# Windowed attention beside a gated MLP on one core: the attention of a chunk done in one piece or in two halves of its tokens

## Chip, cores and metric

The kernel runs on one core of one Trainium2 chip. The metric is the time on the device in microseconds (us); of several runs the median is taken. The time before is 718.12 us, the median of three runs (717.82 to 720.67).

## The reference

The input is one sequence of 2048 tokens of width 1024. It is normalised; the normalised tokens go through an attention with 32 heads of 32, in which each token looks at itself and the seven tokens at distances 2, 4, ... 14 before it, and through a gated MLP of inner width 3584. The output is the input plus attention times silu of the MLP.

```python
qkv = (xn @ wqkv)                       # 3 x 32 heads x 32
W, dil = 8, 2
idx = pos[:, None] - off[None, :]       # off = 0, 2, ... 14
logits = jnp.einsum("bhsd,bhswd->bhsw", q, kg) * scale
logits = jnp.where(mask[None, None, :, :], logits, -1e9)
attn = _softmax(logits, axis=-1)
o = jnp.einsum("bhsw,bhswd->bhsd", attn, vg)
s = o @ wo
g = _silu((_silu(xn @ w1) * (xn @ w3)) @ w2)
return x + s * g
```

## The kernel before

The tokens are worked on in two blocks of 1024, each of two chunks of 512, so there are four chunks (0 to 3). TensorE (PE) does the projections, the MLP and the output projection. Each of these products is a two by two block product done with seven instead of eight partial products, which costs VectorE (DVE) many sums and differences of weights, of inputs and of results; the ones of the first block's MLP weights are kept in HBM (s_dram, t_dram) and loaded again for the second block.

The order of the blocks is: projections q, k, v (qkv_first, qkv_pairs), up projections in 14 steps (up_step), attention of the block's first chunk, down projection (mlp_down), output projection of that chunk (wo). The attention of the block's second chunk stands at the start of the next block, or at the end of the program, and its output projection after the next block's projections. Queries, keys or values that come before they can be used are parked in HBM (put, get).

That is the order in which the operations are written down. The order on each engine is made by a planner (class Plan, lines 43 to 247): each operation is noted with its engine, what it reads and writes, and an assumed cost; PE keeps the written order, and for the other engines `limits` works back from PE to the time by which each operation is due, and `simulate` takes on each engine, whenever it is free, the ready operation that is due first. `plan.lift` moves the due times of a group: for chunks 1 to 3 the softmax and its copies are pulled forward by 60 us (SOFT, line 699). Buffers of a pool are handed out in the written order (`place`, line 72). So a change of the attention can move DVE, ScalarE (ACT) and the DMA queues of SyncE (SP) and GpSimd (POOL), but not PE. An engine runs its list in order: an instruction that waits holds up everything behind it.

The attention of a chunk c (`attention`, line 701) does not use PE. Queries, keys and values lie with the 128 partitions as 32 heads times 4 parts of a head's width, and 8 further values (j) in the free dimension, each for 512 tokens: `qo[:, u, j, :]`, `kT`, `vT`; keys and values have the last 16 tokens of the chunk before in front (HALO, copied by `halo`, line 547).

- Scores (lines 709 to 726): for each of the 8 distances w, the product of q and the shifted k in two instructions of 2048 elements (four j each, `qk`), the sum of the two (`qa`, 2048), then sums of halves (`qb`, 1024; `qc`, 512) into a tile E that holds, for each of four quarters of the tokens, 8 distances of 128 tokens. What is left to sum is across the four partitions of a head.
- Regrouping (lines 734 to 738): four DMAs of 256 KB, two issued by POOL and two by SP, copy E into L so that a partition holds one head and one quarter of the tokens, with the four parts side by side. L takes two of the three buffers of the pool `att`.
- Softmax (lines 739 to 762): three sums of 1024 fp32 elements (`z`), a tree of three maxima (512, 256, 128; `tr`), the difference (`zd`, 1024), the exponential on ACT (line 756, 1024), a tree of three sums, a reciprocal (line 760, 128) and the product (`pb`, 1024).
- Spreading (lines 763 to 766): four DMAs of 256 KB copy the weights back into E, for each of the four partitions of a head.
- Product with v (lines 768 to 792): for each half of the j, 8 products and 7 sums of 2048 elements (`pv`, `pa`), over q in `qo`.

All `tt` operations (sums, products) are recorded at line 365, all copies on ACT at 370, silu at 373, all DMAs at 379, and the matmuls at 356 (some of the down projection at 1070). In the profile att is the pool of attention buffers, k the fp32 buffers for results of PE, mm the banks of PSUM, r the large buffers for weights.

Of the kernel before, what the change touches and what calls it, by code (L numbers as in the profile page):

```python
# [8 lines left out]
FP32 = mybir.dt.float32  # L9
BF16 = mybir.dt.bfloat16  # L10
FP16 = mybir.dt.float16
ACTF = mybir.ActivationFunctionType
ALU = mybir.AluOpType

PE, DVE, ACT, POOL, SP = range(5)
# [229 lines left out]
def kernel(  # L245
# [11 lines left out]
    nc = tc.nc  # L257
    P = 128
    S, D, F = 2048, 1024, 3584
    Dh, W, DIL = 32, 8, 2  # L260
    KT = D // P
    KH = KT // 2
    CH = 512
    BL = 1024
    NB = S // BL
    NST = CH // P
# [3 lines left out]
    HALO = 16  # L270
    NJ = 8
    NR = 4
    NQ = 7
    scale = float(Dh) ** -0.5
# [10 lines left out]
    const = ctx.enter_context(tc.tile_pool(name="const", bufs=1))  # L285
# [11 lines left out]
    maskb = const.tile([P, W, HALO], BF16, name="maskb")  # L297
    kT = const.tile([P, NJ, HALO + CH], BF16, name="kT")
    vT = const.tile([P, NJ, HALO + CH], BF16, name="vT")
    h_sb = const.tile([P, FT, BL], BF16, name="h_sb")  # L300
    h16 = h_sb[:].bitcast(FP16)
    E = const.tile([P, NST, W, P], BF16, name="E")
    qo = const.tile([P, 2, NJ, CH], BF16, name="qo")
    xT = const.tile([P, 2, KT, CH], BF16, name="xT")
    xT16 = xT[:].bitcast(FP16)
# [4 lines left out]
    plan = Plan()  # L310
# [15 lines left out]
        out=ident[:], in_=ident[:], compare_op=ALU.not_equal, fill=1.0,  # L326
# [4 lines left out]
        out=maskb[:], in_=maskb[:], compare_op=ALU.is_ge, fill=-1.0e9,  # L331
# [2 lines left out]
    nc.gpsimd.memset(kT[:, :, 0:HALO], 0.0)  # L334
    nc.gpsimd.memset(vT[:, :, 0:HALO], 0.0)
    warm = plan.pools["k2"][7][:].bitcast(BF16)
    zero = E[:, 0, 0:4, :].rearrange("p w n -> p (w n)")
    nc.vector.memset(warm[:, 0:CH], 0.0)
    nc.vector.memset(zero, 0.0)
    for i in range(12):  # L340
# [22 lines left out]
    def tt(name, fn, o, a, b, rd, wr, n, fast, late=0.0):  # L363
        occ = n / (1920.0 if fast else 960.0) + 0.068
        plan.op(DVE, name, lambda: fn(out=o(), in0=a(), in1=b()), rd, wr, occ, 0.08, late=late)  # L365

    add, sub, mul, mx = (nc.vector.tensor_add, nc.vector.tensor_sub, nc.vector.tensor_mul, nc.vector.tensor_max)
# [8 lines left out]
    def dma(eng, name, o, a, rd, wr, kb, run=1024, late=0.0):  # L376
        e = {SP: nc.sync, POOL: nc.gpsimd, ACT: nc.scalar}[eng]
        occ = {SP: 0.45, POOL: 0.58, ACT: 0.55}[eng]
        plan.op(eng, name, lambda: e.dma_start(out=o(), in_=a()), rd, wr, occ, 0.0, nbytes=kb * 1024, late=late, run=run)  # L379
# [20 lines left out]
    def qo_cells(u, js, gs=range(4)):  # L400
        return [("qo", u, j, g) for j in js for g in gs]
# [297 lines left out]
    SOFT = (0.0, -60.0, -60.0, -60.0)  # L699

    def attention(c):
        u = c % 2
        J4 = [range(0, 4), range(4, 8)]
        r4 = lambda s: s.ap().rearrange("p (j n) -> p j n", j=4)
        if ("q", c) in park:
            get(c, "q")
        if ("k", c) in park:
            halo("k")
            get(c, "k")
        for w in range(W):  # L710
            o = HALO - DIL * w
            pr = []
            for jh in range(2):
                p_t = plan.slot("att", f"p{c}_{w}_{jh}")
                tt(f"qk{c}", mul, lambda p_t=p_t: r4(p_t), lambda jh=jh: qo[:, u, jh * 4:jh * 4 + 4, :],
                   lambda jh=jh, o=o: kT[:, jh * 4:jh * 4 + 4, o:o + CH],
                   qo_cells(u, J4[jh]) + [("k", j) for j in J4[jh]] + ([("k", j, "halo") for j in J4[jh]] if w else []),
                   [p_t], 2048, True)
                pr.append(p_t)
            p0, p1 = pr  # L720
            tt(f"qa{c}", add, lambda p0=p0: r4(p0), lambda p0=p0: r4(p0), lambda p1=p1: r4(p1), [p0, p1], [p0], 2048, True)
            tt(f"qb{c}", add, lambda p0=p0: r4(p0)[:, 0:2], lambda p0=p0: r4(p0)[:, 0:2], lambda p0=p0: r4(p0)[:, 2:4],
               [p0], [p0], 1024, True)
            tt(f"qc{c}", add, lambda w=w: E[:, :, w, :], lambda p0=p0: r4(p0)[:, 0].rearrange("p (q n) -> p q n", n=P),
               lambda p0=p0: r4(p0)[:, 1].rearrange("p (q n) -> p q n", n=P),
               [p0], [("E", w, sq) for sq in range(4)], 512, True)
        if ("v", c) in park:
            halo("v")
            get(c, "v")
        if c == 0:  # L730
            tt("mask", add, lambda: E[:, 0, :, 0:HALO], lambda: E[:, 0, :, 0:HALO], lambda: maskb[:],
               [("E", w, 0) for w in range(W)], [("E", w, 0) for w in range(W)], 128, False)
        plan.lift = SOFT[c]
        L = plan.slot("att", f"L{c}", 2)
        Lv = lambda r: L.ap().rearrange("p (r w n) -> p r w n", r=NR, w=W)[:, r]
        for sq in range(4):
            dma((POOL, SP)[sq % 2], f"L{c}", lambda sq=sq: L.ap()[sq:P:4].rearrange("h (r n) -> h r n", r=NR),
                lambda sq=sq: E[:, sq].rearrange("p w n -> p (w n)"), [("E", w, sq) for w in range(W)], [(L, sq)], 330, 2048)
        zf = lambda s: s.ap().bitcast(FP32)
        z = plan.slot("att", f"z{c}")  # L740
        zv = lambda: zf(z).rearrange("p (w n) -> p w n", w=W)
        LC = [(L, sq) for sq in range(4)]
        tt(f"z{c}", add, zv, lambda: Lv(0), lambda: Lv(1), LC, [z], 1024, False)
        tt(f"z{c}", add, zv, zv, lambda: Lv(2), LC + [z], [z], 1024, False)
        tt(f"z{c}", add, zv, zv, lambda: Lv(3), LC + [z], [z], 1024, False)
        zm = plan.slot("att", f"zm{c}")
        zt = lambda s: zf(s)[:, 0:512].rearrange("p (w n) -> p w n", w=4)

        def tree(t, op):
            tt(f"tr{c}", op, lambda: zt(t), lambda: zv()[:, 0:4], lambda: zv()[:, 4:8], [z], [t], 512, False)  # L750
            tt(f"tr{c}", op, lambda: zt(t)[:, 0:2], lambda: zt(t)[:, 0:2], lambda: zt(t)[:, 2:4], [t], [t], 256, False)
            tt(f"tr{c}", op, lambda: zt(t)[:, 0:1], lambda: zt(t)[:, 0:1], lambda: zt(t)[:, 1:2], [t], [t], 128, False)

        tree(zm, mx)
        tt(f"zd{c}", sub, zv, zv, lambda: zt(zm)[:, 0:1].to_broadcast([P, W, P]), [z, zm], [z], 1024, False)
        plan.op(ACT, f"exp{c}", lambda: nc.scalar.activation(out=zf(z), in_=zf(z), func=ACTF.Exp, scale=scale),  # L756
                [z], [z], 1.07, 0.11, table="exp")
        zs = plan.slot("att", f"zs{c}")
        tree(zs, add)
        plan.op(DVE, f"rec{c}", lambda: nc.vector.reciprocal(out=zt(zs)[:, 0], in_=zt(zs)[:, 0]), [zs], [zs], 0.87)  # L760
        pb = plan.slot("att", f"pb{c}")
        pbv = lambda: pb.ap()[:, 0:1024].rearrange("p (w n) -> p w n", w=W)
        tt(f"pb{c}", mul, pbv, zv, lambda: zt(zs)[:, 0:1].to_broadcast([P, W, P]), [z, zs], [pb], 1024, False)
        for sq in range(4):
            dma((POOL, SP)[sq % 2], f"E{c}", lambda sq=sq: E[:, sq].rearrange("p w n -> p (w n)"),
                lambda sq=sq: pb.ap()[sq:P:4, 0:1024].unsqueeze(1).to_broadcast([32, NR, 1024]),
                [pb], [("E", w, sq) for w in range(W)], 330, 2048)
        plan.lift = 0.0
        for jh in range(2):
            js = slice(jh * 4, jh * 4 + 4)  # L770
            A = lambda js=js: qo[:, u, js, :]
            Ac = qo_cells(u, J4[jh])

            def pv(dst, wr, w, jh=jh, js=js):
                o = HALO - DIL * w
                q4 = lambda a: a.rearrange("p j (q n) -> p j q n", n=P)
                tt(f"pv{c}", mul, lambda: q4(dst()), lambda: E[:, :, w, :].unsqueeze(1).to_broadcast([P, 4, NST, P]),
                   lambda: q4(vT[:, js, o:o + CH]),
                   [("E", w, sq) for sq in range(4)] + [("v", j) for j in J4[jh]]
                   + ([("v", j, "halo") for j in J4[jh]] if w else []), wr, 2048, True)  # L780

            pv(A, Ac, 0)
            B = plan.slot("att", f"B{c}")
            pv(lambda B=B: r4(B), [B], 1)
            tt(f"pa{c}", add, A, A, lambda B=B: r4(B), Ac + [B], Ac, 2048, True)
            for w0 in (2, 4, 6):
                B, C = plan.slot("att", f"B{c}"), plan.slot("att", f"C{c}")
                pv(lambda B=B: r4(B), [B], w0)
                pv(lambda C=C: r4(C), [C], w0 + 1)
                tt(f"pa{c}", add, lambda B=B: r4(B), lambda B=B: r4(B), lambda C=C: r4(C), [B, C], [B], 2048, True)  # L790
                tt(f"pa{c}", add, A, A, lambda B=B: r4(B), Ac + [B], Ac, 2048, True)


    def xn_sums(hold=False):
# [515 lines left out]
    for st in range(NST):  # L1310
        x_load(0, st, x0)
    plan.op(ACT, "warm", lambda: nc.scalar.activation(out=scr[:], in_=eps_t[:], func=ACTF.Sqrt), [], [], 0.2,
            table="sqrt")
# [125 lines left out]
```

## Time and profile before

| | |
|---|---|
| median of three runs | 718.12 us (717.82 to 720.67) |
| the profiled execution | 718.92 us, span of its instructions 716.9 us |
| PE busy | 706.6 us, 3407 matmuls |
| DVE busy | 661.9 us, 901 instructions |
| ACT busy | 389.4 us, 668 instructions |
| DMA | 150.56 MB, mean 210 GB/s |
| DVE on the attention's tile att | 313.9 us |
| copies E to att, att to E | 32 of 256 KB, 2.4 to 7.3 us from issue to landing |

The span runs from the first to the last instruction; what is around it (2.0 us) is start and end of the execution. An engine's busy time counts each moment once, also where two instructions overlap. A group's line gives the number of instructions, their total, the mean of one in ns, and the idle time of the engine just before them with what ended it. A timeline's line gives start, length, engine, line, operation, tiles, shape and how many, and in brackets the idle time before.

The four chunks' attention lies so in the trace (first to last instruction on DVE): chunk 0 from 48.0 to 246.8 us, chunk 1 from 244.4 to 414.5, chunk 2 from 414.4 to 552.0, chunk 3 from 547.3 to 689.1.

### The profile page before, as it was taken

What the parts mean: (1) busy time and instruction counts of PE and PEld (TensorE: products, weight loads), DVE (VectorE), ACT (ScalarE), POOL (GpSimd) and SP (SyncE); (2) the same over time, 40 slices, a digit from 0 to 9 for tenths busy, and PEclk for the clock granted to TensorE, in tenths of its full rate; (3) what the DMA queues carried; (4) which work ended last, traced back from release to release, by engine and by line L of the source; (5) the groups of instructions that cost most, each with busy time, mean ns of one, the idle gap of its engine ahead of it and who ended that gap; (6) DMA issues with size and microseconds to landing.
All of it is one profiled execution on the core that took longest, in us unless ns stands there. A gap on an engine that the chain in (4) does not pass through costs nothing.

```text
span 716.9 us, 9340 instructions
## 1 busy us (share of the span) xinstructions
PE 706.6 (99%) x3407; PEld 352.3 (49%) x3462; DVE 661.9 (92%) x901; ACT 389.4 (54%) x668; POOL 25.4 (4%) x54
## 2 busy tenths in 40 slices
PE   8999999999999999999999999999999999999997
PEld 5655544444444444744555554444444444455443
DVE  6999999987999999979799999975999997999968
ACT  6755465567565697534535354657565654422233
POOL 0011100100000000000000000000000000000000
PEclk9999999999999999999999999999999999999999
DMA  8579985866544849695554559897537346437523
GB/s 315 214 247 388 370 295 167 283 207 215 183 169 150 305 127 241 144 299 184 192 156 157 176 183 321 267 307 225 194 109 254 113 157 213 155 128 239 177 73 103
DMA packets 127262, 150.56 MB, mean 210 GB/s; under 512 B 12400, under 2 KB 104176, under 8 KB 122864
## 3 DMA queue, kind: packets, MB, share of 16 engines
q1 hardware_dynamic: 113312, 121.58, 52.3%
q0 software_dynamic: 5312, 26.22, 9.3%
q10 hardware_dynamic: 8592, 2.16, 2.2%
q8 instruction: 27, 0.44, 0.3%
q14 instruction: 19, 0.16, 0.1%
HBM read 106.95 MB, written 32.51 MB: 195 GB/s over the span
## 4 chain that ended last, share of the span: by engine, by line
PE 97%; DVE 1%; DMA 1%; issue 1%; SPq 0%; DVEq 0%
PE mm L356 93%; PE mm L1070 3%; DVE r L365 1%; DMA r<-in_A_wqkv_dram 1%; PE mm L508 0%; SPq L379 0%; DVEq L1434 0%; DVEq L365 0%
## 5 line engine op out<-in xcount | busy, mean ns | idle before, releaser
L356 PEld LDWEIGHTS <-r 128*128 128x128 f16 (+1 forms) x2288 | 239.9, 107 | 245.8 <-DMA r<-in_A_wqkv_dram 2.3
L356 PE MATMUL mm<-xs,r 128*128 128x512 f16 x1280 | 295.2, 379 | 0.0
L356 PE MATMUL mm<-xT,r 128*128 128x512 bf16 (+1 forms) x968 | 224.4, 369 | 3.4 <-DMA r<-in_A_wqkv_dram 1.3
L370 ACT COPY k<-mm 128x512 f32<-128x512 f32 (+1 forms) x200 | 115.0, 579 | 87.0 <-PE mm L356 73.0
L356 PE MATMUL mm<-r,h_sb 128*128 128x512 bf16 (+1 forms) x694 | 153.7, 379 | 0.5
L365 DVE TENSOR_TENSOR att<-att 128x2048 bf16<-128x2048 bf16 (+4 forms) x132 | 124.0, 950 | 7.2 <-ACT att L756 5.2
L356 PEld LDWEIGHTS <-h_sb 128*128 128x128 f16 (+1 forms) x800 | 78.2, 98 | 93.2
L370 ACT COPY mm<-mm 128x512 f32<-128x512 f32 (+1 forms) x92 | 51.5, 563 | 81.7 <-PE mm L356 69.5
L365 DVE TENSOR_TENSOR att<-qo,kT 128x2048 bf16<-128x2048 bf16 x64 | 76.8, 1215 | 0.0
L365 DVE TENSOR_TENSOR att<-E,vT 128x2048 bf16<-128x2048 bf16 x56 | 66.2, 1216 | 0.0
L365 DVE TENSOR_TENSOR h_sb<-mm,k 128x512 bf16<-128x512 f32 x96 | 62.8, 680 | 0.9 <-PE mm L356 0.3
L365 DVE TENSOR_TENSOR r<-r,r 128x1024 f16<-128x1024 bf16 (+6 forms) x76 | 58.9, 784 | 1.9 <-DMA r<-in_A_wqkv_dram 1.3
L373 ACT ACTIVATE k<-k 128x512 bf16<-128x512 f32 x56 | 34.7, 630 | 45.1 <-DVE k L365 45.0
L365 DVE TENSOR_TENSOR k<-mm,k 128x512 f32<-128x512 f32 x72 | 47.8, 683 | 9.8 <-PE mm L356 9.5
L365 DVE TENSOR_TENSOR h_sb<-h_sb,k 128x1024 bf16<-128x1024 bf16 x56 | 37.0, 683 | 14.0 <-ACT k L370 14.0
L373 ACT ACTIVATE h_sb<-mm 128x512 bf16<-128x512 f32 x60 | 35.8, 598 | 18.1 <-PE mm L356 18.0
L370 ACT CAST k<-mm 128x512 bf16<-128x512 f32 x56 | 32.5, 587 | 12.4 <-PE mm L356 12.4
L365 DVE TENSOR_TENSOR qo<-qo,att 128x2048 bf16<-128x2048 bf16 x32 | 38.9, 1215 | 0.0
L365 DVE TENSOR_TENSOR h_sb<-h_sb 128x512 f16<-128x512 bf16 (+1 forms) x72 | 37.4, 561 | 1.0 <-DMA h_sb<-in_B_w_dram 0.8
L365 DVE TENSOR_TENSOR r<-r 128x1024 f16<-128x1024 bf16 (+2 forms) x36 | 27.8, 790 | 0.6 <-DMA r<-t_dram 0.6
L356 PE MATMUL mm<-h_sb 128*128 128x512 f16 x96 | 22.4, 379 | 0.1
L373 ACT ACTIVATE xs<-k 128x512 bf16<-128x512 f32 x8 | 5.0, 630 | 20.6 <-DVE k L365 20.6
(98 smaller groups left out, 378.9 us busy)
## 6 DMA issues: line engine op xcount, KB each, us to landing
r<-in_B_w_dram SPq DMA_DIRECT2D x42, 512.0 KB, 4.0
s_dram<-r POOLq DMA_DIRECT2D x14, 1024.0 KB, 5.5
r<-t_dram SPq DMA_DIRECT2D x16, 896.0 KB, 6.6
r<-s_dram SPq DMA_DIRECT2D x14, 1024.0 KB, 4.9
r<-in_A_wqkv_dram SPq DMA_DIRECT2D x11, 1024.0 KB, 6.8
r<-in_B_w_dram SPq DMA_DIRECT2D x12, 896.0 KB, 4.7
h_sb<-in_B_w_dram SPq DMA_DIRECT2D x14, 512.0 KB, 11.2
t_dram<-h_sb POOLq DMA_DIRECT2D x14, 512.0 KB, 6.9
```

Source lines behind the costliest of these rows:

```text
L356: nc.tensor.matmul(cut(ps.ap()), lhsT=lhs[k](), rhs=cut(rhs[k]()), start=(first and k == 0), stop=(last and k == n - 1), skip_group_check= ...
L365: plan.op(DVE, name, lambda: fn(out=o(), in0=a(), in1=b()), rd, wr, occ, 0.08, late=late)
L370: plan.op(ACT, name, lambda: nc.scalar.copy(out=o(), in_=a()), rd, wr, occ, 0.11)
L373: plan.op(ACT, name, lambda: nc.scalar.activation(out=o(), in_=a(), func=ACTF.Silu), rd, wr, occ, 0.11, table="silu")
L1070: nc.tensor.matmul(ps.ap()[:, col * 256:(col + 1) * 256], lhsT=lhs[k](), rhs=r()[:, k, :], start=first and k == 0, stop=False, skip_group_ ...
```

## The change

The attention of a chunk is done for the first 256 tokens and for the second 256, one behind the other in each step: scores and regrouping of half 0, scores and regrouping of half 1; softmax and spreading of half 0, then of half 1; product with v of half 0, then of half 1. E has the shape [P, 2 halves, 4 quarters of a half, W, 64]. A product of scores takes all 8 j of 256 tokens at once (2048 elements), so its sums have 1024, 512 and 256 elements. L takes one buffer for each half; the softmax of a half works on 512 columns and keeps its intermediate results in one buffer. The copies have 128 KB each, in contiguous runs of 1 KB, and there are twice as many.

```diff
-    E = const.tile([P, NST, W, P], BF16, name="E")
+    E = const.tile([P, 2, 4, W, CH // 8], BF16, name="E")
...
-        for w in range(W):
...
-                tt(f"qk{c}", mul, lambda p_t=p_t: r4(p_t), lambda jh=jh: qo[:, u, jh * 4:jh * 4 + 4, :],
...
-            tt(f"qa{c}", add, lambda p0=p0: r4(p0), lambda p0=p0: r4(p0), lambda p1=p1: r4(p1), [p0, p1], [p0], 2048, True)
...
+        tok = [slice(h * HN, (h + 1) * HN) for h in H2]
...
+        for h in H2:
+            for w in range(W):
+                p = plan.slot("att", f"p{c}_{w}_{h}")
+                kw, kc = kv("k", w, h)
+                pj = lambda a, b, p=p: (lambda: r8_(p)[:, a:b])
+                tt(f"qk{c}", mul, pj(0, 8), lambda h=h: qo[:, u, :, tok[h]], kw, qc_(h) + kc, [p], 2048, True)
+                tt(f"qa{c}", add, pj(0, 4), pj(0, 4), pj(4, 8), [p], [p], 1024, True)
+                tt(f"qb{c}", add, pj(0, 2), pj(0, 2), pj(2, 4), [p], [p], 512, True)
+                row = lambda j, p=p: (lambda: r8_(p)[:, j].rearrange("p (q n) -> p q n", q=4))
+                tt(f"qc{c}", add, lambda w=w, h=h: E[:, h, :, w, :], row(0), row(1), [p], ec(h, [w]), 256, True)
...
+            plan.lift = SOFT[c]
+            L.append(plan.slot("att", f"L{c}_{h}"))
+            for q in Q4:
+                dma((POOL, SP)[q % 2], f"L{c}",
...
+                    lambda q=q, h=h: E[:, h, q].rearrange("p w n -> p (w n)"), ec(h, q=[q]), [(L[h], q)], 165, 1024)
+            plan.lift = 0.0
...
-        L = plan.slot("att", f"L{c}", 2)
...
-        tt(f"z{c}", add, zv, lambda: Lv(0), lambda: Lv(1), LC, [z], 1024, False)
...
-        for sq in range(4):
-            dma((POOL, SP)[sq % 2], f"E{c}", lambda sq=sq: E[:, sq].rearrange("p w n -> p (w n)"),
...
+        for h in H2:
...
+            tt(f"z{c}", add, zv, Lv(0), Lv(1), LC, [zz], 512, False)
+            tt(f"z{c}", add, zv, zv, Lv(2), LC + [zz], [zz], 512, False)
+            tt(f"z{c}", add, zv, zv, Lv(3), LC + [zz], [zz], 512, False)
...
+            tree(mx)
+            tt(f"zd{c}", sub, zv, zv, wide, [zz], [zz], 512, False)
+            plan.op(ACT, f"exp{c}", lambda zf=zf: nc.scalar.activation(out=zf(0, 512), in_=zf(0, 512), func=ACTF.Exp, scale=scale),
+                    [zz], [zz], 0.6, 0.11, table="exp")
+            tree(add)
+            plan.op(DVE, f"rec{c}", lambda zf=zf: nc.vector.reciprocal(out=zf(512, 576), in_=zf(512, 576)), [zz], [zz], 0.47)
...
+            for q in Q4:
+                dma((POOL, SP)[q % 2], f"E{c}", lambda q=q, h=h: E[:, h, q].rearrange("p w n -> p (w n)"),
+                    lambda q=q, pbv=pbv: pbv()[q:P:4].unsqueeze(1).to_broadcast([32, NR, 512]),
+                    [zz], ec(h, q=[q]), 165, 1024)
         plan.lift = 0.0
-        for jh in range(2):
...
+        for h in H2:
+            A = lambda h=h: qo[:, u, :, tok[h]]
...
```

The planner makes a new order from this. On PE it is the same as before. On DVE 898 planned operations become 1042. On ACT the eight exponentials of 512 elements stand one by one between other work in chunks 0, 2 and 3, each with a load of its table before it and of silu's after it; in chunk 1 the two stand together.

## The prediction

> **What bounds it now.** I read the totals of the page first, then the chain of work that ended last, then the waits of TensorE (PE) alone, and only then VectorE (DVE), on which the whole change lies.
>
> ```profile
> PE 706.6 (99%) x3407; PEld 352.3 (49%) x3462; DVE 661.9 (92%) x901; ACT 389.4 (54%) x668; POOL 25.4 (4%) x54
> ...
> PE 97%; DVE 1%; DMA 1%; issue 1%; SPq 0%; DVEq 0%
> ```
>
> ```profile
> PE mm L356 <- DMA r<-in_A_wqkv_dram: 1.3, 2, 0.9
> PE mm L341 <- DVE k L338: 1.2, 1, 1.2
> PE mm L508 <- DVE r L443: 0.3, 1, 0.3
> ```
>
> The second fence is the complete list of what PE waits for: 2.8 us, all in the first stages. The chain names PE from 25 us to the last matmul at 712.2 us, in stretches without a hole, and the granted clock is 1.00 in every window up to 700 us. So PE sets the end, and neither attention nor anything else of DVE holds it up anywhere. A time saved on DVE has nowhere to go; a time added on DVE costs nothing as long as each result still comes before the matmul that needs it.
>
> What the change can fill is idle time of DVE. The timeline of DVE shows where it stood:
>
> ```profile
> 475.28 0.69 DVE L365 TENSOR_TENSOR h_sb<-h_sb,k 128x1024 bf16<-128x1024 bf16 x1 [4.24 <-ACT k L370]
> ...
> 488.06 1.16 DVE L365 TENSOR_TENSOR att<-att 128x512 f32<-128x512 f32 x2 [3.02 <-ACT att L756]
> ...
> 499.45 0.69 DVE L365 TENSOR_TENSOR h_sb<-h_sb,k 128x1024 bf16<-128x1024 bf16 x1 [4.19 <-ACT k L370]
> ```
>
> These three are chunk 2: attention is blocked first on the regrouping copies (issued 468.1, used 475.9), then on the exponential, then on the spreading copies (issued 492.9, used 500.9), and DVE has too little else to do. All of DVE's gaps of over 1 us between 60 us and the last attention instruction at 689.1 come to 31.7 us. PE waited in none of them.
>
> **The change, part by part.** PE's instructions and their order are the same, one by one; so are the sums, the stores and the loads of weights. What changes is on DVE, ACT and the queues of SP and POOL.
>
> *Scores.* Durations come from the groups kept apart by shape:
>
> ```profile
> L365 DVE TENSOR_TENSOR att<-qo,kT 128x2048 bf16<-128x2048 bf16 x64 | 76.8, 1215 | 0.0
> L365 DVE TENSOR_TENSOR att<-att 128x1024 bf16<-128x1024 bf16 x32 | 21.7, 681 | 0.0
> L365 DVE TENSOR_TENSOR E<-att 128x512 bf16<-128x512 bf16 x32 | 13.1, 415 | 0.0
> L365 DVE TENSOR_TENSOR r<-r,xs 128x256 bf16<-128x256 bf16 x2 | 0.5, 282 | 0.0
> L365 DVE TENSOR_TENSOR att<-att 128x1024 f32<-128x1024 f32 x12 | 14.7, 1222 | 0.3
> L365 DVE TENSOR_TENSOR att<-att 128x512 f32<-128x512 f32 x8 | 5.5, 684 | 5.2 <-ACT att L756 5.2
> ```
>
> Before, a chunk takes 16 products of 1.215 us and 8 times (1.215 + 0.681 + 0.415): 37.9 us. After, the same 16 products and 16 times (0.681 + 0.415 + 0.282): 41.5 us. Same elements, 24 instructions more. These durations overlap, though: two independent instructions of 1.215 us take 2.35 us, so each starts 80 ns before the end of the one ahead. Net +3.6 - 24 x 0.08 = **+1.6 us** per chunk. The rows hold no run of 64 elements spread over four dimensions; but weight sums that step in runs of 4 take 1.218 us for 2048 elements and the products with v in runs of 128 take 1.216, so I price the new shapes by size alone.
>
> ```profile
> 579.99 2.35 DVE L365 TENSOR_TENSOR att<-qo,kT 128x2048 bf16<-128x2048 bf16 x2
> ...
> 477.63 2.48 DVE L365 TENSOR_TENSOR att<-att 128x1024 f32<-128x1024 f32 x2
> ```
>
> *Softmax.* Before: 5 x 1.22, two trees of 0.684 + 0.420 + 0.286, a reciprocal of 0.948: 9.8 us. After: 10 x 0.684, four trees of 0.420 + 0.286 + 0.22 (the last an estimate from the 286 ns of 128 and the 420 ns of 256), two reciprocals of 0.55 (estimated from 948 ns at 128 and 154 ns at 1): 11.6 us. Less 12 overlaps of 0.08: **+0.85 us**. The second line above is a pair in which the second reads what the first wrote: 2.48 is 2 x 1.222 + 0.03, so a dependent neighbour loses 0.11 us. By the printed order attention has 20 such neighbours before and 31 after: +1.3 us in all, **+0.3** per chunk.
>
> *Product with v.* Still 30 instructions of 2048 elements a chunk: 0.
>
> Sum: 2.75 us a chunk, 11 us in all, of which DVE has 55 free. It lies beside PE's matmuls. Two dates decide whether it stays there. The second chunk's attention ends at 414.5; the first sum that needs all of it precedes its matmul (423.5) by 7.3 us, so it may end at 421.8. The fourth ends at 689.1; the next sum started at 696.6, held by matmuls of the chunk before it, with 2.0 us to spare, so it may end at 698.6. If no gap were filled at all, two chunks' extra (5.5 us) put these ends at 420.0 and 694.6: still in time. With gaps filled they come earlier than now. So **0** on the path. Without this cover the whole 11 us would show.
>
> *Exponential.* Four become eight, each with half the elements: 0.63 us by the 512-element activations beside 1.056. In the changed order chunks 0, 2 and 3 load the tables twice, chunk 1 once as now: 6 loads more.
>
> ```profile
> 485.68 1.28 ACT L756 ACT_TABLE_LOAD   x1
> 486.98 1.06 ACT L756 ACTIVATE att<-att 128x1024 f32<-128x1024 f32 x1
> ...
> 489.50 1.28 ACT L373 ACT_TABLE_LOAD   x1
> ```
>
> A detour now costs ACT 2 x 1.283 + 1.056 = 3.6 us, and the evictions behind this one still came 0.7 us before their matmul at 492.6. A new one is 3.2 us, with other work between the two: **0**, at most 3.2 + 3.2 - 3.6 - 0.7 = 2.1 us a chunk if two fall together. [...]
>
> *Copies.* L and E go in 64 DMAs of 128 KB instead of 32 of 256 KB: 16 more issues on SP (0.59 us each) and 16 more on POOL (0.56). They land 2.4 to 7.3 us after the issue now. Stores of 256 KB take 2.4 and of 128 KB 1.8, so a half could land 0.6 us sooner; behind a 512 KB weight load it lands no sooner. I take the same latency, and 0. On SP, in chunk 1, four copies of L now stand ahead of a load from t_dram that had one ahead of it and one behind; such loads land 4.7 us or more ahead of use, against three issues more (1.8 us). Elsewhere a copy waits at the head of SP until its half is done, with weight loads behind it; the tightest of these have 1.6 us. [...]
>
> *Start and tail.* DVE's order is the same up to 48 us, and the last 28 us have the same instructions. Nothing to gain there.
>
> The profiled execution took 718.92 us (span 716.9, and 2.0 around it), 0.8 over the median of the three runs, 718.12. With 0 on the path and 0.3 for margins that shrink, the median should be **718.4**.
>
> **The rivals.**
>
> *DVE comes late and PE waits (slower).* For it: windows 200:250, 350:450 and 650:675 are full; the smallest margins of DVE ahead of a matmul are 0.3 us at 301.1, 1.3 at 289.8 and 1.75 at 449.4. Against it: the priority work stands in the same places, and attention fills between. It decides when the halved instructions don't overlap. If all 36 added ones of a chunk cost 0.182 us (0.068 plus 0.114) and nothing is filled, a chunk takes 6.7 more: the ends are 427.9 and 702.5, late by 6.1 and 3.9, which gives 729. At half of that (4.7 a chunk) the ends are 423.9 and 698.5: 2.1 late, 720.5. I put it at 724.
>
> *ACT's detours fall together.* Three chunks by 2.1 us: 725. Against it: DVE work of a half lies between two exponentials.
>
> *A copy holds up weight loads on SP.* The half that is waited for is late by DVE's own delay; one such wait past the 1.6 us margin, by the 4 us a load takes to land: 718.4 + 2.4, about 721.
>
> *Faster.* The gaps are filled and the ends of attention come earlier; PE needs neither. Only a hole in PE could give time back, and after 25 us there is none: 718.0 at best. That the planner does not lay the halves behind each other (chunk 1's L copies all stand together) ends in the forecast's time too.
>
> **How the numbers follow.** A difference of 0.5% (3.6 us) is about what this measurement can tell from none. Forecast and its equal-time rivals 0.72; DVE late 0.15; ACT 0.06; SP 0.04, all three counted as slower; faster by over 0.5% 0.03. The range runs from 717.4 (0.4 under the fastest run shown, 717.8, which is about how far the two faster ones lie apart) to 724.0, the middle of the first rival.
>
> **What would show it.** Right: PE's list of waits stays under 4 us, the chain stays 97% PE, DVE's busy time is 671 to 675 us in about 1045 instructions, 7 table loads of the exponential instead of 4, the idle time of DVE around 475, 488 and 499 shrinks, and it grows before 694. Wrong: a wait of PE for DVE h_sb, k or mm at line 365, or for ACT k or mm at line 370; halved shapes over their price; copies that land after 8 us.

## The result, and the profile after

The changed kernel takes 742.64 us in the median of 4 runs (741.49 to 744.57), the kernel before 718.71 (717.82 to 720.67) beside it: a ratio of 1.034, with a 95% interval of 1.031 to 1.037. The forecast was 718.4 us with a range up to 724.0. It was wrong by 24 us, on the side to which it gave a quarter of the chance.

The totals of the page after, and its chain of the work that ended last:

```profile
PE 713.7 (96%) x3407; PEld 354.3 (48%) x3462; DVE 671.3 (90%) x1045; ACT 389.5 (52%) x678; POOL 34.2 (5%) x70
...
PE 8%; DVE 4%; issue 0%; DVEq 0%
```

DVE is busy 671.3 us in 1045 instructions, as forecast. But its share falls from 92 to 90%, since the span has grown by 25.1 us, from 716.9 to 742.0. The chain no longer runs back through PE to the start: it covers the last 12% of the span and breaks off. All of PE's waits (total us, times, longest):

```profile
PE mm L356 <- ACT k L370: 12.4, 3, 9.2
PE mm L1074 <- DVE mm L365: 4.0, 3, 2.8
PE mm L356 <- DVE h_sb L365: 1.7, 3, 0.7
PE mm L341 <- DVE k L338: 1.2, 1, 1.2
PE mm L508 <- DVE r L443: 0.7, 1, 0.7
PE mm L356 <- DMA r<-in_A_wqkv_dram: 0.6, 1, 0.6
```

They come to 20.6 us where there were 2.8. PE is also busy 7.1 us longer (706.6 to 713.7) with the same matmuls. The waits have grown by 17.8 us; 17.8 and 7.1 are 24.9 of the 25.1 us, so two questions are left: why PE waits, and why its work takes longer.

The largest wait leads to the first one's cause. These are rows of the timelines of chunk 0, engine by engine (start, length, instruction, and in brackets the idle time before and what ended it):

```profile
155.39 0.69 DVE L365 TENSOR_TENSOR att<-att 128x512 f32<-128x512 bf16 x1 [5.87 <-DMA att<-E]
158.80 3.19 DVE L365 TENSOR_TENSOR att<-att 128x512 f32<-128x512 f32 x6 [2.72 <-DMA att<-E]
...
175.93 0.29 DVE L365 TENSOR_TENSOR att<-att 128x128 f32<-128x128 f32 x1 [3.29 <-DMA E<-att]
179.00 0.22 DVE L365 TENSOR_TENSOR att<-att 128x64 f32<-128x64 f32 x1 [2.77 <-DMA E<-att]
```

```profile
149.54 7.10 SPq L379 DMA_DIRECT2D att<-E  x2
```

```profile
156.37 0.55 POOL L379 DMA_DIRECT2D att<-E  x1 [6.01 <-DVE att L365]
```

```profile
158.77 1.28 ACT L764 ACT_TABLE_LOAD   x1 [7.42 <-DMA att<-E]
```

```profile
165.09 3.55 PE L356 MATMUL mm<-xs,r 128*128 128x512 f16 x8 [9.18 <-ACT k L370]
...
181.61 3.10 PE L356 MATMUL mm<-xs,r 128*128 128x512 f16 x8 [2.62 <-ACT k L370]
```

The instruction at 155.39 is the first sum of half 0's softmax. It needs half 0's four L copies, the last of which had landed at 148.61 (landings are taken from the trace, by each copy's semaphore). It started 0.28 us after the landing of two copies of *half 1*, issued at 149.54 and 149.81 (landed 154.78 and 155.11). The other two copies of half 1 then were issued at 156.10 and 156.37, as soon as that sum had ended at 156.08: SP's two issues took 7.10 us, and POOL's row names DVE as what it waited for. The second sum, at 158.80, followed the landing of those two (158.72). So a sum of half 0 waits for copies of half 1, copies of half 1 for that sum, and the next sum for these copies. None of this is in the data. At 175.93 and 179.00 the same happens with the spreading: the tree of half 1 waits for the E copies of half 0, which only read half 0's result. In chunk 2 the three idle times that the prediction showed around 475, 488 and 499 us (4.24, 3.02 and 4.19 us, ended by ACT) have given way to three that a copy ends: 2.69 us before 488.74, 4.70 before 506.43 and 2.30 before 509.16.

What is common to all of them is the tile. L, the softmax's intermediate results and the spread source all lie in the one wide tile att, in different thirds of it, and a copy touches every fourth partition of its third (`[q:P:4]`). The planner keeps its own books by buffer and lays half 0's sums beside half 1's copies; the waits in the program follow the order in which these come out and the tile. In the kernel before, no copy of a chunk stands between two parts of the chunk's softmax, so nothing there could wait in this way.

### The profile page after: what moved, and what is told of

Its sections match the earlier page's. It is cut to its first block, busy times and chain, and to the rows that moved or that the text cites. A ratio compares the mean times of both kernels' runs of the same rounds, so it can differ in the third digit from the quotient of the medians.

```text
span 742.0 us, 9547 instructions
## 1 busy us (share of the span) xinstructions
PE 713.7 (96%) x3407; PEld 354.3 (48%) x3462; DVE 671.3 (90%) x1045; ACT 389.5 (52%) x678; POOL 34.2 (5%) x70
## 5 line engine op out<-in xcount | busy, mean ns | idle before, releaser
L356 PEld LDWEIGHTS <-r 128*128 128x128 f16 (+1 forms) x2288 | 240.7, 108 | 262.8 <-issue 20.6
L356 PE MATMUL mm<-xs,r 128*128 128x512 f16 x1280 | 298.5, 382 | 14.2 <-ACT k L370 12.4
L365 DVE TENSOR_TENSOR att<-att 128x1024 bf16<-128x1024 bf16 (+8 forms) x240 | 133.4, 589 | 33.1 <-DMA E<-att 16.7
L370 ACT COPY k<-mm 128x512 f32<-128x512 f32 (+1 forms) x200 | 113.4, 580 | 76.4 <-PE mm L356 59.6
L370 ACT CAST k<-mm 128x512 bf16<-128x512 f32 x56 | 32.3, 590 | 8.3 <-PE mm L356 8.0
L379 POOL DMA_DIRECT2D att<-E x16 | 8.8, 557 | 312.2 <-DVE E L365 306.2
```

The costliest lines, as they stand in the source:

```text
L356: nc.tensor.matmul(cut(ps.ap()), lhsT=lhs[k](), rhs=cut(rhs[k]()), start=(first and k == 0), stop=(last and k == n - 1), skip_group_check= ...
L370: plan.op(ACT, name, lambda: nc.scalar.copy(out=o(), in_=a()), rd, wr, occ, 0.11)
```

## The experiments

Each ran beside the kernel before on the same chip; the ratios are to that kernel.

| kernel | us, median | ratio, 95% interval | PE's waits, us |
|---|---|---|---|
| after | 742.64 | 1.034 (1.031 to 1.037) | 20.6 |
| e1: three tiles for att | 719.17 | 1.0019 (1.0010 to 1.0028) | 4.0 |
| e2: copies of both halves together | 719.00 | 1.0013 (1.0003 to 1.0024) | 2.6 |
| e2a: only the L copies together | 726.17 | 1.0115 (1.0101 to 1.0129) | 7.4 |
| e3: exponential off the softmax | 739.92 | 1.0304 (1.0288 to 1.0319) | 20.3 |
| e4: scores alone in halves | 719.24 | 1.0018 (1.0002 to 1.0034) | 2.0 |
| e5: wide tile, blocks of partitions | 727.30 | 1.0132 (1.0118 to 1.0146) | 9.6 |
| e6: three tiles and blocks | 726.30 | 1.0099 (1.0079 to 1.0119) | 9.8 |
| e7: before, with blocks | 722.11 | 1.0048 (1.0033 to 1.0063) | 4.5 |

**e1, three tiles.** My theory was now the false waits; the rivals were the amount of work on DVE, the table loads, and the number of copies. One line tells them apart, since it moves no instruction:

```diff
-    plan.wide = {"att": (const.tile([P, 12 * CH], BF16, name="att"), 4 * CH)}
+    plan.pools["att"] = [const.tile([P, 4 * CH], BF16, name=f"att{i}") for i in range(3)]
```

> The changed kernel with the three buffers of att as three tiles in place of one wide one; every instruction stands in the same place on every engine, and only waits differ. Theory 1 (false waits: a copy between E and one buffer of the wide tile att is taken to touch the whole tile, so that the softmax of one half waits for the other half's copies): PE's waits fall from 18 to under 4 us, PE busy from 713.7 to about 707, 718 to 721 us. Theory 2 (too much work on DVE, halved instructions and dependent neighbours) and theory 3 (table loads of the exponential between PE's evictions) change nothing here: 738 us or more. Theory 4 (twice as many copies of half the size clog the queues): also 735 or more.

Measured 719.17 us. The same first sum of half 0, on DVE's timeline of this run:

```profile
149.98 0.69 DVE L365 TENSOR_TENSOR att<-att 128x512 f32<-128x512 bf16 x1 [0.41 <-DVE E L365]
```

It starts 5.4 us earlier, 0.2 us after the landing of half 0's own last L copy (149.80); the copies of half 1, which land from 156.16 on, no longer hold it. PE's busy time is back at 706.9 us. All of the loss but 1.4 us is gone (0.0019 of 718; 0.7 to 2.0 by the interval), with every added instruction, table load and copy still there: the three rivals together explain no more than that rest. The order on DVE, ACT and POOL is the changed kernel's, instruction by instruction.

**e2, copies together.** The wide tile stays, and the order is changed instead:

```diff
-            LC = [(L[h], q) for q in Q4]
+            LC = [(L[x], q) for x in (H2 if h == 0 else (1,)) for q in Q4]
...
+            z.append(zz)
+        for h in H2:
+            pbv = lambda zz=z[h]: zz.ap()[:, 1536:2048]
             for q in Q4:
...
-                    [zz], ec(h, q=[q]), 165, 1024)
+                    z, ec(h, q=[q]), 165, 1024)
```

> The wide tile stays, but the copies of the two halves are put together: the first sum of half 0 is planned behind all L copies, and the E copies of both halves behind both halves' softmax. Shapes, instruction counts, eight exponentials, 64 copies of 128 KB as in the changed kernel. Theory 1: no copy lies between the softmax of the two halves, so nothing is left to wait for falsely: 718 to 722 us, PE's waits under 5 us. Theories 2 and 4: 735 or more. Theory 3: between, since two exponentials may share a load of their table.

Measured 719.00 us (ratio 1.0013). Here half 0's first sum waits for all eight L copies, more than in the changed kernel, and all changes together cost 0.9 us (0.2 to 1.7 by the interval). The wait itself is not what is dear: the planner now knows of it and gives DVE other work, which in chunk 0 lies between 149.9 us and that sum's start at 158.0. The loss goes here with the wide tile where it was, so the buffers' place in memory is not its cause either.

**e2a, one side only.** The first line of that diff alone.

> As the run before, but only the L copies are put together; the E copies of half 0 still start before half 1's softmax is over, so that the false waits on the spreading side stay and those on the regrouping side go. Theory 1: the stall of 9.2 us on PE near 165 us goes, stalls of up to 3 us as at 181 us may stay in each of chunks 0 to 3: 719 to 730 us. Theories 2 to 4: 735 or more.

Measured 726.17 us, and on DVE's timeline the two waits of the spreading side are still there:

```profile
177.09 0.42 DVE L365 TENSOR_TENSOR att<-att 128x256 f32<-128x256 f32 x1 [3.94 <-DMA E<-att]
180.15 0.55 DVE L365 TENSOR_TENSOR att<-att 128x128 f32<-128x128 f32 x2 [2.63 <-DMA E<-att]
```

So the regrouping side costs 742.6 - 726.2 = 16.5 us and the spreading side 726.2 - 719.0 = 7.2. The planner's order differs a little between these kernels, so this is a division of the loss, not an exact price of each wait.

**e3, exponential off the softmax.** PE waited for ACT, and ACT stood 7.42 us at the exponential's table load. I took that for the way by which DVE's delay reached PE.

```diff
-            ... nc.scalar.activation(out=zf(0, 512), in_=zf(0, 512), func=ACTF.Exp, scale=scale),
+            ... nc.scalar.activation(out=scr[:], in_=scr[:], func=ACTF.Exp, scale=scale),
```

> The changed kernel in the same order, but the exponential works on one column that nothing else uses, so the scores are not exponentiated: the eight table loads stay, and nothing on ScalarE waits for the softmax any more. DVE's false waits stay. If PE stalls because ScalarE stands in line behind the exponential with PE's evictions behind it (theory 1, by way of ScalarE): PE's wait for ACT k falls from 12.4 to under 2 us, and the time to 721 to 730 us. If the stall reaches PE by DVE's own late work: 735 or more. If the table loads themselves cost the time (theory 3): 740.

Measured 739.92 us: what I had taken for the way (721 to 730 us) was wrong. By itself this time would also fit the price of the table loads (740), but e1 keeps all of them and had ruled that out. PE's waits changed their name:

```profile
PE mm L356 <- DVE h_sb L365: 13.3, 5, 6.9
PE mm L1074 <- DVE mm L365: 3.8, 3, 2.4
```

DVE's false waits stay: it stands 5.95 us before the first sum of half 0 at 155.91 us and 3.17 before the next at 159.78. Behind these, in the order of the changed kernel and of e1, stands a sum into h_sb that starts at 167.75 us (at 158.68 in e1), and PE waits 6.94 us for DVE's h_sb, until 168.48. Freed from the one road, the delay comes by the other. The wait on ACT adds some 2 to 3 us to it at most (742.6 - 739.9; the intervals of the ratios touch).

**e4, scores alone.** The kernel before with only the scores in halves (products of 8 j by 256 tokens, the rest as it was).

```diff
+        for h in range(2):
+            for w in range(W):
+                o = HALO - DIL * w + h * 256
+                p = plan.slot("att", f"p{c}_{w}_{h}")
...
+                tt(f"qc{c}", add, lambda w=w, h=h: E[:, 2 * h:2 * h + 2, w, :], row(0), row(1), [p],
+                   [("E", w, 2 * h), ("E", w, 2 * h + 1)], 256, True)
```

> The kernel before with the scores alone in halves: products of 8 j by 256 tokens, sums of 1024, 512 and 256 elements (24 instructions more a chunk, +1.6 us a chunk on DVE); regrouping, softmax, spreading and product with v as before, 32 copies of 256 KB, no copy between two parts of a softmax. The prediction's price of this part on the path is 0: 717.5 to 720 us, DVE busy 666 to 671 us, PE's waits under 4 us. If more and smaller instructions on DVE cost by themselves: 722 or more.

Measured 719.24 us, with DVE busy for 668.2 us in place of 661.9: 6.3 us more, 1.6 a chunk. PE's waits (2.0 us) show nothing of it on the path; by the ratio it costs 1.3 us, and 2.4 at most.

**e5, blocks of partitions.** If the tile is at fault, which part of it? This kernel keeps the wide tile and the order and changes only how a copy walks over its partitions. The softmax works row by row, so it does not matter which row a head's quarter takes.

```diff
-                    lambda q=q, l=L[h]: l.ap()[q:P:4].rearrange("h (r n) -> h r n", r=NR),
+                    lambda q=q, l=L[h]: l.ap()[32 * q:32 * q + 32].rearrange("h (r n) -> h r n", r=NR),
...
-                    lambda q=q, pbv=pbv: pbv()[q:P:4].unsqueeze(1).to_broadcast([32, NR, 512]),
+                    lambda q=q, pbv=pbv: pbv()[32 * q:32 * q + 32].unsqueeze(1).to_broadcast([32, NR, 512]),
```

> The changed kernel with the one wide tile, the same order on every engine and the same copies, but a copy's 32 partitions of att are a block (32q to 32q+31) in place of every fourth (q, q+4, ...); the softmax works row by row, so the output is the same. If it is the strided walk over partitions that makes a copy seem to touch all three buffers (theory 1 in full): as with three tiles, 718 to 721 us, PE's waits under 4 us. If the wide tile alone does it, whatever the walk: 738 us or more. If the copies land later because a block of partitions moves slower than a strided set, the median from issue to landing rises above 4.5 us (E to att) or 3 us (att to E); without false waits that stays hidden.

Measured 727.30 us: between the two. The pattern of chunk 0 is gone (PE's stall there is 1.2 us in place of 9.2), so the walk matters. But I had written that slower copies would stay hidden, and they did not. The DMA lists of e1 and of e5 (KB each, median us from issue to landing), and e5's first wait of PE:

```profile
att<-E SPq DMA_DIRECT2D x16, 128.0 KB, 3.6
att<-E POOLq DMA_DIRECT2D x16, 128.0 KB, 4.5
```

```profile
att<-E SPq DMA_DIRECT2D x16, 128.0 KB, 6.9
att<-E POOLq DMA_DIRECT2D x16, 128.0 KB, 6.5
```

```profile
PE mm L356 <- DMA r<-in_A_wqkv_dram: 4.3, 2, 3.9
```

From E to att, a block of 32 partitions lands 2.0 to 3.3 us later than every fourth one. In chunk 1, SP then issued the loads of wqkv behind the E copies at 346.6 us, 5.4 later than in e1 (341.2), and PE stood 3.9 us for one of them.

**e6 and e7.** Did blocks with the wide tile leave false waits, or were the copies all of it? e6 has e1's line and e5's lines together; e7 has e5's lines in the kernel before.

> Three tiles for att (as in the run that came to 719.2) and blocks of 32 partitions in the copies (as in the run that came to 727.3). If what the blocks with the wide tile still lost against three tiles (8 us) is the slower landing of the copies (6.5 to 6.9 us from issue in place of 3.6 to 4.5 from E to att), it is lost here too: 725 to 729 us, again with a wait of PE for a wqkv load near 355 us. If it is false waits that the blocks left behind in the wide tile: 718 to 721 us.

> The kernel before, with blocks of 32 partitions in the copies of 256 KB and everything else as it was; the output is the same. Its copies have no work of the same softmax behind or ahead of them that could wait falsely. If blocks move slower whatever their size, the median landing rises from 4.0 to 4.7 to 6.5 us or more, and the time stays at 717.5 to 720 where that is covered, or rises to 721 to 727 where a load of weights on SP comes late.

```diff
-                lambda sq=sq: pb.ap()[sq:P:4, 0:1024].unsqueeze(1).to_broadcast([32, NR, 1024]),
+                lambda sq=sq: pb.ap()[32 * sq:32 * sq + 32, 0:1024].unsqueeze(1).to_broadcast([32, NR, 1024]),
```

e6 took 726.30 us: with blocks, three tiles gain 2.4 us over e5 (1.0099 against 1.0132) where without them they gained 23. So most of what e5 lost against e1 is the slow landing (6 us by e6 against e1), and at most the 2.4 us can be false waits that the blocks left behind. Even these need not be: from 355.77 to 362.59 us e5's granted clock was 0.50 with PE busy for 5.66 us, half of which is 2.8, and e6's stayed at 1.00. As expected, e6 has its wait for a wqkv load near 355 us (2.42 us, ending at 354.95). How a program's waits are made from a tile and a walk no run here shows, only that either change takes them away.

In e7 the four medians of landing rose from between 4.0 and 4.7 us to between 6.6 and 8.3, and the time rose to 722.11. The late load that I had expected behind such a time isn't there: PE waits 1.1 us for wqkv (1.3 before), and the largest addition is 1.4 us in three waits for DVE mm. What makes the rest of the 3.4 us that the ratio gives stays open.

No kernel here beats the one before. In e1 the idle times of DVE of over 1 us between 60 us and the end of attention come to 16.6 us in place of 31.7, and attention ends at 685.0 us in place of 689.1, so the halves do fill gaps; but PE, busy 706.9 us, has no use for it.

## Why the prediction was wrong, step by step

**What bounds the kernel.** That PE set the end before was right, and that a result which comes late costs the whole delay followed from it.

**Scores and softmax.** Right. The groups of the changed kernel, shape by shape (count | total us, mean ns | idle before):

```profile
L365 DVE TENSOR_TENSOR att<-att 128x1024 bf16<-128x1024 bf16 x64 | 42.1, 681 | 0.0
L365 DVE TENSOR_TENSOR E<-att 128x256 bf16<-128x256 bf16 x64 | 16.0, 281 | 0.0
...
L365 DVE TENSOR_TENSOR att<-att 128x64 f32<-128x64 f32 x16 | 3.3, 220 | 2.9 <-DMA E<-att 2.8
```

The new shapes cost what the sizes said, the 64 elements 220 ns as estimated. DVE's busy time grew by 9.4 us. From e4 the scores have 1.6 of it a chunk (forecast 1.6) and the rest 0.8 (forecast 0.85, with 0.3 more for dependent neighbours).

**Two dates.** The margin argument held where its premise did: in e1 the second and fourth chunk's attention end at 412.0 and 685.0 us, earlier than before (414.5 and 689.1), as the prediction said for filled gaps. In the changed kernel they end at 426.5 and 708.5. The premise was that DVE's added time is work. It was mostly waiting: 32.3 us in ten waits for copies between E and att, not all of them false.

**Exponential.** Table loads rose from 14 to 20, the 6 more that were forecast. Their price of 0 stands: e1 has them all and loses 1.4 us over everything. The rival in which ACT's detours fall together (725) was wrong in mechanism; ACT's 7.42 us ended, by their row, with a copy that the exponential does not need; after its table load it stood until 162.02 us for the difference on DVE, which the same copies had held up. e3 shows that without ACT's wait PE stalls nearly as long.

**Copies: this step failed.** "They land 2.4 to 7.3 us after the issue now ... I take the same latency, and 0." The latency was right in the medians: the four are 2.4 to 4.4 us, against 4.0 to 4.7 before. SP's four L copies of chunk 1 took 8.9 to 10.5 us, over the 8 us that the prediction had named as a sign; but e1 has four of 8.8 to 10.2 and loses 1.4 us over everything. From POOL the shortest copy took 2.30 us for 128 KB and 3.03 for 256 KB, from SP 2.04 and 2.38, so half the bytes landed 0.7 and 0.3 us sooner at the shortest. What was missing is not a duration. The prediction asked how long a copy takes and who needs it by its data. It did not ask which other instructions touch the same tile between a copy's issue and its landing. Both facts were there to be read: one wide tile behind all three buffers, and a copy's walk over every fourth partition of it. The change put copies of one half between the sums of the other, and with that the price went from 0 to about 23 us (742.6 - 719.2 is 23.5; by the ratios, each taken on its own chip, it is 22.8).

**The rivals.** "DVE comes late and PE waits" had the right symptom, and PE's list shows the waits it named (ACT k, DVE h_sb, DVE mm). But its condition was that halved instructions don't overlap, which gave 720.5 to 729 (36 instructions of 0.182 us are 6.6 and not 6.7, and the upper end comes to 728; the choice of 724 does not hang on it); e1 shows that these, with all else that was added, cost 1.4 us. "A copy holds up weight loads on SP" did not happen in the changed kernel and did in e5 and e6, by the slower landing: PE stood 3.9 and 2.4 us for a load of wqkv and, just behind it, 1.2 and 2.0 us for DVE's sums of weights. With e5's slower matmuls these are most of the 8 and 6 us that the two lose against e1, in place of the 2.4 at which the rival was priced. The signs listed for a wrong forecast included PE's waits for ACT k and DVE h_sb; the sign that would have led straight to the cause, DVE waiting for a copy of the other half, was not among them.

**A second term that was missing.** The prediction priced a stall at its own length. PE's matmuls took 7.1 us of the 25.1 longer, and about 6.2 of that, by the estimate below, comes from three stretches at half the granted clock behind the stalls.

## What to carry to other kernels

When a change lays copies of one part beside the work of another, list for each tile who touches it between a copy's issue and its landing: here a wait came from the tile and the walk over its partitions where the data ask for none (5.87 us before one sum, 0.41 with a tile for each buffer). A planner that orders by its own books makes such a wait dear, because it puts nothing there to fill it; a tile for each buffer (719.17 us), or an order in which copies and sums don't alternate (719.00), took away nearly all of it in place of the changed kernel's 742.64. And where PE sets the end, price a stall of some microseconds with the slower matmuls behind it: here, by the estimate below, 1.7, 1.7 and 2.8 us behind stalls of 9.18, 2.62 and 2.82 us.

## What the runs showed of the hardware

**PE's clock after a stall.** Stretches of the changed kernel after the stalls of 9.18 us (ends at 165.09) and 2.62 us (ends at 181.61): length, PE's busy time, granted clock, DMA share, GB/s.

```profile
165.00:168.40 3.40, 3.31 (x8) 0.50 0.01 2
168.40:179.00 10.60, 10.54 (x48) 1.00 0.59 208
181.60:184.60 3.00, 2.99 (x9) 0.59 0.02 5
```

After the long stall the matmuls start every 427 ns in place of 216, for 3.4 us. After the one of 2.62 us the first three come at 215 to 326 ns and the next eight at 427. In all, by the trace's records of the clock, it is granted at 0.50 from 158.24 to 168.48 us, from 182.13 to 185.54 and, behind a stall of 2.82 us that ends at 669.74, from 670.24 to 677.06. PE is busy there for 3.39, 3.41 and 5.62 us; half of that, about 1.7, 1.7 and 2.8, is an estimate of what the slower clock cost beside the stalls themselves.

The length of a stall does not decide this alone: one of 2.42 us in e6 left the matmuls after it at 215 to 273 ns, and one of 2.38 us in e3 was followed by a clock of 0.50. The times at which the clock changes tell more. In every trace here with more than one change they lie whole multiples of 3.41 us apart (from 158.24 to 670.24 us it is 150 times that). Cut into stretches of this length that end at a change, PE's busy time in the last one before each of the three halvings was as follows (columns as above; a fourth, at 741.92, stands behind all work):

```profile
154.83:158.24 3.41, 1.08 (x5) 1.00 0.27 77
178.72:182.13 3.41, 0.79 (x5) 1.00 0.49 140
666.83:670.24 3.41, 0.59 (x6) 1.00 0.96 327
```

The stall of 2.42 us in e6 falls into two such stretches, counted back from that trace's one change at 726.0 us, and neither is followed by a halving:

```profile
350.53:353.95 3.42, 2.01 (x10) 1.00 1.01 380
353.95:357.36 3.41, 1.95 (x8) 1.00 0.68 253
```

In e3 the stall of 2.38 us lies in one stretch, with 1.03 us of work (666.16 to 669.57 us). In the ten traces each stretch at full clock with 1.08 us of work or less was followed by half the clock, and none with 1.78 us or more; between these two there is no case. So what counts in these traces is how a stall lies in the stretches: of two stalls of about 2.4 us, e3's was followed by a clock of 0.50 and e6's was not.

**Which partitions a copy takes.** With 32 partitions in a block, the medians from E to att were 6.9 and 6.5 us, with every fourth one 3.6 and 4.5, both for 128 KB at the same places in the same order. Why a block lands later no run here shows.
